# Two GpSimd copies moved behind a subtraction, and wider warm-up products on TensorE, in an attention and expert-layer kernel

## The chip, the cores and the metric

The kernel runs on one core of one Trainium2 chip. The metric is the time of one execution on the device in microseconds (us). The kernel before took 209.54 us, the median of three runs (209.17 to 210.24). One further execution was recorded by the hardware profiler: it took 208.29 us, of which 206.5 us lie between its first and its last instruction (the span). All places in time below are counted from the start of that span.

## The reference, cut to what matters

```python
B, H, S, Ns, D = 8, 8, 512, 32, 64
scores  = x @ state^T / 8                 # per batch and head: 512 x 32
a       = exp(scores - max) / sum         # over the 32 states
xread   = a @ state                       # 512 x 64
scores2 = state @ x^T / 8                 # 32 x 512
a2      = exp(scores2 - max) / sum        # over the 512 positions
sread   = a2 @ x                          # 32 x 64
h       = concat(xread, sread)            # 544 rows, heads side by side: 512 wide
out     = gelu(h @ w_in) @ w_out          # 512 -> 2048 -> 512
```

The result has 8 x 544 rows of 512 float32 values.

## The kernel before

The eight batches follow one another, and in each the work of the next one is prepared. TensorE (PE in the profile) is fed in program order. The kernel folds `state @ w_in` into a matrix P, so that `gelu` takes P times the transposed attention weights (`mm1`). The second product of each batch, gelu times `w_out`, is done by Strassen's scheme: seven half-size products, named "3", "4", "5", "1", "2", "7", "6" in the order in which they run, with sums and differences before (`g_sum`) and after them.

Three parts matter here. The first is the combination behind the products. [...]

```python
def c22(b):
    xs[b, "v"] = c_tile("v")
    o = xs[b, "o", 1]
    nc.gpsimd.tensor_tensor(out=xs[b, "v"], in0=xs[b, "q"], in1=o[:, :, :NH], op=ALU.subtract)  # L588
    nc.vector.tensor_tensor(out=o[:, :, NH:], in0=xs[b, 3], in1=xs[b, "v"], op=ALU.add)         # L591, reads bank 3
    x_out(b, 1)

def X(b, name):
    bank = {"3": 0, "4": 1, "5": 0, "2": 1, "1": 2, "6": 3, "7": 2}[name]
    ...                                     # sixteen products into the bank (L569)
    elif name == "5":
        nc.scalar.copy(out=o, in_=ps)                                                           # L615
        nc.gpsimd.tensor_tensor(out=xs[b, "u"], in0=xs[b, "s34"], in1=o, op=ALU.subtract)       # L618
    elif name == "2":
        nc.scalar.copy(out=xs[b, "o", 1][:, :, :NH], in_=ps)                                    # L620
        c22(b)
    elif name == "1":
        nc.vector.tensor_tensor(out=xs[b, "q"], in0=ps, in1=xs[b, "s34"], op=ALU.add)           # L624
    elif name == "7":
        nc.vector.tensor_tensor(out=xs[b, "o", 0][:, :, :NH], in0=ps, in1=xs[b, "u"], op=ALU.add)  # L626, reads bank 2
```

The second part is GpSimd's copies of x. Each batch needs x in two arrangements: `x4` (`rearr`, L219), whose transpose feeds the scores, and `xo` (`rearr_ones`, L229), x with columns of ones between, so that one product gives both the sum of `a2` and `a2 @ x` (`sread`). There are two `xo` tiles: batch b uses `xos[b % 2]`. `hold_for` is a copy of one column that only keeps a following load from being issued early.

```python
def rearr_ones(b):
    A = atts[b]
    eng = nc.vector if b < 2 else nc.gpsimd
    src = xbs[b].rearrange("p (t c) (j d) -> p t c j d", t=2, d=D)
    for t in range(2):
        eng.tensor_copy(out=A.xo[:, :, :, 2 + 64 * t:66 + 64 * t].rearrange("p j c d -> p c j d"),
                        in_=src[:, t])                                                          # L229
```

The loop over batches has eight steps p in each:

```python
for b in range(2, B):
    nb = b + 1
    for p in range(8):
        k = 16 * b + 2 * p
        ...
        if p == 7 and nb < B:
            srt(b)                          # a transpose on TensorE (L403), reads srm
        M(k, k + 1)                         # mm1 (L460), each followed by gelu on ScalarE (L467)
        if b == 2 and p in (0, 3):
            pmat(2, 2 + p // 3)             # P of batch 2: products L416
        if p < 5:
            ...
            X(b - 1, "45127"[p])            # the products of the batch before
            if p < 3:
                g_sum(b - 1, "127"[p])
        if p == 0 and b + 3 < B:
            hold_for(b, 0)
            load_x(4 if b == 2 else b + 3)
        if p == 2 and b == 2:
            rearr_ones(3)                   # the line that moves
        if p == 6 and b == 2:
            hold_for(b, 12)
            load_x(5)
        if p == 0 and nb + 1 < B:
            begin(nb + 1)
            rearr(nb + 1)
        ...
        if p == 5:
            g_sum(b, "6")
            sread(b)                        # (L379) reads xo of batch b
            p_run(nb, (0, 1), ((0, 1), (3, 2)))  # P of the next batch: L416 into banks 0, 1, then 3, 2; then four copies to SBUF (L427, L428)
            sread_out(b)                    # L392, L393: writes srm
            if nb + 1 < B:
                rearr_ones(nb + 1)
        if p == 6:
            X(b, "3")
        if p == 7:
            p_run(nb, (2, 3), ((1, 2), None))
            X(b, "6")
```

The third part is the warm-up. At seven places of the first 11 us TensorE multiplies a tile of zeros by itself, to stay busy while it has nothing to do; nobody reads the result. The calls ask for 31, 3, 2, 2, 2, 12 and 3 products.

```python
warm = persist.tile([128, 128], BF16, name="warm")
nc.vector.memset(warm, 0.0)                 # L92

def keep_warm(n):
    ps = otile([128, 512], "warm_ps")
    for _ in range(n):
        nc.tensor.matmul(ps[:, 0:128], lhsT=warm, rhs=warm, start=True, stop=True)   # L147
```

Of the kernel before, what the change touches and what calls it, by code (L numbers as in the profile page):

```python
# [10 lines left out]
BF16 = mybir.dt.bfloat16  # L11
# [6 lines left out]
def kernel(  # L18
# [8 lines left out]
    nc = tc.nc  # L27

    B, H, S, D = x.shape
    _, _, NS, _ = state.shape  # L30
# [8 lines left out]
    persist = ctx.enter_context(tc.tile_pool(name="persist", bufs=1))  # L39
# [15 lines left out]
    def otile(shape, name, at=None):  # L55
        if at is None:
            at = turn[0] % 4
            turn[0] += 1
        return ps_o.tile(shape, FP32, name=name, tag=f"o{at}")
# [17 lines left out]
    sb0 = persist.tile([128, 2, 2, 2, NS], BF16, name="sb0")  # L77
    gate = persist.tile([128, HC], FP32, name="gate")
    hold = persist.tile([128, 1], BF16, name="hold")
    warm = persist.tile([128, 128], BF16, name="warm")  # L80
    xos = [persist.tile([128, SJ, HC, 132], BF16, name=f"xo_{i}") for i in range(2)]
    x4s = [persist.tile([128, SJ, HC, 128], BF16, name=f"x4_{i}") for i in range(2)]

# [59 lines left out]

    def keep_warm(n):
        ps = otile([128, 512], "warm_ps")
        for _ in range(n):
            nc.tensor.matmul(ps[:, 0:128], lhsT=warm, rhs=warm, start=True, stop=True)  # L147


    def state_prep(b0, b1):  # L150
# [73 lines left out]
# [5 lines that stand above are left out]
            eng.tensor_copy(  # L229
                out=A.xo[:, :, :, 2 + 64 * t:66 + 64 * t].rearrange("p j c d -> p c j d"),  # L230
                in_=src[:, t],
            )
# [37 lines left out]
    def xtr_dma(b):  # L270
        A = atts[b]
        nc.sync.dma_start_transpose(
            out=A.xT.rearrange("p j c n -> p (j c) n"),
            in_=A.x4.rearrange("p j c n -> p (j c n)"),
        )
# [41 lines left out]
    def scores(b, half):  # L317
        A = atts[b]
        if half == 0:
            begin_e(b)  # L320
        pt = ps_f.tile([128, SJ, 2, 2, NS], FP32, name="pt", tag="f")
        for ci in range(2):
            c = 2 * half + ci
            for j in range(SJ):
                nc.tensor.matmul(  # L325
                    pt[:, j, :, ci, :],
                    lhsT=A.xT[:, j, c, :],
                    rhs=sbd[:, b, c, :],
                    start=True,
                    stop=True,  # L330
                )
        nc.scalar.activation(
            out=A.e[:, :, 64 * half:64 * half + 64],
            in_=pt.rearrange("p j t c n -> p (j t) (c n)"),
            func=AF.Exp,
            scale=scale,
        )

    def norm(b, half):
        A = atts[b]  # L340
        G = SJ * 2
        hs = slice(64 * half, 64 * half + 64)
        e4 = A.e[:, :, hs].rearrange("p g (c n) -> p g c n", n=NS)
        cs = att.tile([128, G, 2], FP32, name="cs", tag="cs")
        nc.vector.reduce_sum(out=cs, in_=e4, axis=AX.X)  # L345
        ics = att.tile([128, G, 2], FP32, name="ics", tag="ics")
        nc.vector.reciprocal(out=ics, in_=cs)  # L347
        nc.vector.tensor_tensor(  # L348
            out=A.a[:, :, hs].rearrange("p g (c n) -> p g c n", n=NS),
            in0=e4,  # L350
            in1=ics[:, :, :].to_broadcast((128, G, 2, NS)),
            op=ALU.mult,
        )
# [11 lines left out]
    def atr_dma(b):  # L365
        A = atts[b]
        A.AT = att.tile([128, SJ, 2, 128], BF16, name="AT", tag="AT")
        nc.sync.dma_start_transpose(
            out=A.AT.rearrange("p j t n -> p (j t) n"), in_=A.a
        )  # L370
# [29 lines left out]
    def srt(b):  # L400
        A = atts[b]
        ps = ps_f.tile([128, HC, NS], BF16, name="srT", tag="f")
        nc.tensor.transpose(  # L403
            ps.rearrange("p c n -> p (c n)"), A.srm.rearrange("q t d -> q (t d)"), ident
        )
        nc.vector.tensor_copy(out=XSR[:, :, :, b], in_=ps)  # L406
# [3 lines left out]
    def p_mm(b, f, tiles):  # L410
        if b not in Ps:
            Ps[b] = att.tile([128, 2, d_ff], BF16, name="P", tag="P")
        ps = [tiles([128, 512], "p_ps") for t in range(2)]
        for c in range(HC):
            for t in range(2):
                nc.tensor.matmul(  # L416
                    ps[t][32 * c:32 * c + 32, :],
                    lhsT=sbd[64 * t:64 * t + 64, b, c, 32 * t:32 * t + 32],
                    rhs=w_in_bf[64 * t:64 * t + 64, c, f * 512:(f + 1) * 512],
                    start=True,  # L420
                    stop=True,
                )
        return ps
# [6 lines left out]
    def pmat(b, f):  # L430
        p_copy(b, f, p_mm(b, f, ftile))
# [347 lines left out]
    def p_run(b, fs, banks, copy=None):  # L779
        done = []  # L780
        for f, at in zip(fs, banks):
            it = iter(at or ())
            tiles = (lambda shape, name: otile(shape, name, next(it))) if at else ftile
            done.append((b, f, p_mm(b, f, tiles)))
        for x in done:
            (copy or p_copy)(*x)
# [5 lines left out]
    def hold_for(b, m):  # L792
        nc.gpsimd.tensor_copy(out=hold, in_=gs[b][:, m, 0:1])


    def M(*ms):
        for m in ms:
            mm1(m // MC, m % MC)
# [5 lines left out]
    begin(0)  # L804
    begin_e(0)
    keep_warm(31)
    cast0(0)
    st0 = state0()
# [38 lines left out]
    for ms in ((0, 1), (2, 3)):  # L847
        for t in range(2):
            for m in ms:
                nc.tensor.matmul(  # L850
                    hps[m],
                    lhsT=Ps[0][:, t, m * 128:(m + 1) * 128],
                    rhs=atts[0].AT[:, :, t, :],
                    start=(t == 0),
                    stop=(t == 1),
# [81 lines left out]
# [4 lines that stand above are left out]
            if p == 1 and nb < B:  # L941
                scores(nb, 0)
                scores(nb, 1)
            if p in (2, 3) and nb < B:
                norm(nb, p - 2)
            if p == 3 and nb + 1 < B:
                xtr_dma(nb + 1)
            if p == 5 and nb < B:
                atr_dma(nb)
            if p == 7 and nb < B:  # L950
                srt(b)
                if nb == B - 1:
                    srt(nb)
            M(k, k + 1)
            if b == 2 and p in (0, 3):
                pmat(2, 2 + p // 3)
            if b == 2 and p == 1:
                w_sums(4)
            if p < 5:
                if p == 0:  # L960
                    g_sum(b - 1, "5")
                X(b - 1, "45127"[p])
                if p < 3:
                    g_sum(b - 1, "127"[p])
            if nb == B and p < 4:
                for m in range(4 * p, 4 * p + 4):
                    mm1_sr(m)
            if p == 0 and b + 3 < B:
                hold_for(b, 0)
                load_x(4 if b == 2 else b + 3)  # L970
            if p == 2 and b == 2:
                rearr_ones(3)
            if p == 6 and b == 2:
                hold_for(b, 12)
                load_x(5)
# [3 lines that stand above are left out]
            if nb == B:  # L979
                if p == 4:  # L980
                    r_homes()
                    r_sum("5")
                    r_sum("2")
                if p == 5:
                    g_sum(b, "6")
                    R("3")
                    r_sum("1")
                    R("4")
                    r_sum("6")
                    r_sum("7")  # L990
                if p == 6:
                    R("5")
                    X(b, "3")
                    R("2")
                    R("1")
                if p == 7:
                    R("6")
                    X(b, "6")
                continue
            if p == 5:  # L1000
                g_sum(b, "6")
                reads = (b, nb) if nb == B - 1 else (b,)
                for r in reads:
                    sread(r)
                p_run(nb, (0, 1), ((0, 1), (3, 2)))
                for r in reads:
                    sread_out(r)
                if nb + 1 < B:
                    rearr_ones(nb + 1)
            if p == 6:  # L1010
                X(b, "3")
            if p == 7:
                p_run(nb, (2, 3), ((1, 2), None))
                X(b, "6")
    b = B - 1
# [40 lines left out]
```

The softmax here doesn't subtract the row's maximum and nothing guards it: scores larger than these inputs give would overflow.

## Time and profile before

| | before |
|---|---|
| time, median of three runs | 209.54 us |
| span of the profiled execution | 206.5 us |
| mean granted TensorE clock | 0.998 |
| GpSimd copies L229 (to `xo`) | 12, 1279 ns mean, 15.0 us |
| GpSimd differences L618 (`u`), L588 (`v`) | 6 each, 1493 and 1402 ns mean |
| chain that ended last, share of PE | 82% |

A line of a timeline reads: start, duration, engine, line of the kernel, operation, tile written <- tiles read, shape, and xN where N equal instructions stand together; a bracket at the end gives the idle time of the engine before it and what ended it. A line of the waits reads: who waited, for whom, us in total, times, longest. Matmuls are pipelined: the duration of a group of them includes the last one's way through the array, so two groups can overlap, and the time that a group costs TensorE is read from its start to the start of the next group. DVE is VectorE, ACT is ScalarE, POOL is GpSimd, PEld is TensorE's weight load.

### The profile page before, as it was taken

How to read it: one execution, taken by the hardware profiler on the slowest of the kernel's cores; microseconds unless marked ns; L12 is line 12 of the kernel's file. 1: busy time of each engine (PE TensorE's matmuls, PEld its weight loads, DVE VectorE, ACT ScalarE, POOL GpSimd, SP SyncE). 2: the span in 40 equal slices, each digit the busy share in tenths (PEclk: the TensorE clock that was granted, in tenths of full speed). 3: DMA queues.
4: the chain of work that ended last, by engine and by line, in shares of the span. 5: the costliest groups of instructions: out<-in, count | busy, mean ns of one | idle time of the engine just before them, and what ended most of it. 6: DMA issues, size and time to landing. Idle time of an engine off the chain costs nothing.

```text
span 206.5 us, 4827 instructions
## 1 busy us (share of the span) xinstructions
PE 198.2 (96%) x2022; PEld 136.1 (66%) x2027; DVE 142.3 (69%) x227; ACT 134.2 (65%) x242; POOL 69.1 (33%) x74
## 2 busy tenths in 40 slices
PE   8699999999999899999999999999999999999992
PEld 7445444455667467766776677577765887878891
DVE  2954886997795868976797767765778533183971
ACT  3864877798885569666967596678758376744020
POOL 8964303724259605370627502520220020200000
PEclk9999999999999999999999999999999999999999
DMA  6999999697358687751783606340115000030134
GB/s 203 183 176 204 206 198 200 139 186 155 44 110 105 203 105 103 153 170 36 85 172 129 77 3 141 122 97 0 56 68 138 0 23 31 0 152 3 51 115 144
DMA packets 40535, 23.16 MB, mean 112 GB/s; under 512 B 21825, under 2 KB 39105, under 8 KB 40513
## 3 DMA queue, kind: packets, MB, share of 16 engines
q0 software_dynamic: 13952, 8.10, 28.7%
q1 hardware_dynamic: 25872, 14.36, 27.6%
q10 hardware_dynamic: 688, 0.39, 0.6%
q8 instruction: 16, 0.26, 0.5%
q14 instruction: 7, 0.05, 0.1%
HBM read 17.30 MB, written 8.91 MB: 127 GB/s over the span
## 4 chain that ended last, share of the span: by engine, by line
PE 82%; POOL 5%; DVE 5%; issue 3%; DMA 2%; ACT 1%; SPq 0%; POOLq 0%; DVEq 0%; ACTq 0%
PE xp L569 35%; PE hp L460 23%; PE p_ps L416 4%; PE hps L501 3%; PE op L514 3%; PE op L486 3%; PE rp L745 3%; DMA x0f<-in_x_dram 2%; PE xp L675 2%; PE pt L325 1%; POOL xo L229 1%; POOL x L219 1%; POOL u L618 1%; PE sr L379 1%; DVE P L428 1%
## 5 line engine op out<-in xcount | busy, mean ns | idle before, releaser
L467 ACT ACTIVATE g<-hp 128x512 bf16<-128x512 f32 x124 | 67.3, 604 | 28.4 <-PE hp L460 21.4
L460 PE MATMUL hp<-AT,P 128*128 128x512 bf16 x248 | 63.6, 379 | 0.0
L569 PEld LDWEIGHTS <-gsum 128*128 128x128 bf16 x528 | 51.2, 98 | 13.1 <-issue 2.1
L563 DVE TENSOR_TENSOR gsum<-g 128x2048 bf16<-128x2048 bf16 x35 | 45.5, 1317 | 0.1
L569 PE MATMUL xp<-ws,gsum 128*128 128x256 bf16 x304 | 36.3, 273 | 0.0
L460 PEld LDWEIGHTS <-P 128*128 128x128 bf16 x248 | 22.9, 98 | 19.9 <-issue 2.8
L569 PE MATMUL xp<-ws,g 128*128 128x256 bf16 x224 | 26.8, 273 | 0.0
L569 PE MATMUL xp<-w_out_bf,gsum 128*128 128x256 bf16 x224 | 26.6, 273 | 0.0
L428 DVE CAST P<-p_ps 128x512 bf16<-128x512 f32 x30 | 19.6, 684 | 8.7 <-PE p_ps L416 8.6
L569 PEld LDWEIGHTS <-g 128*128 128x128 bf16 x224 | 21.8, 98 | 5.1 <-issue 0.2
L618 POOL TENSOR_TENSOR u<-s,oh 128x512 f32<-128x512 f32 x6 | 9.0, 1493 | 41.1 <-ACT oh L615 41.1
L427 ACT CAST P<-p_ps 128x512 bf16<-128x512 f32 x30 | 16.9, 600 | 5.7 <-PE p_ps L416 5.4
L219 POOL COPY x<-xb 128x1024 bf16<-128x1024 bf16 x12 | 13.6, 1163 | 15.8 <-DMA xb<-in_x_dram 15.8
L229 POOL COPY xo<-xb 128x1024 bf16<-128x1024 bf16 x12 | 15.0, 1279 | 4.6 <-PE sr L379 4.6
L588 POOL TENSOR_TENSOR v<-q,oh 128x512 f32<-128x512 f32 x6 | 8.4, 1402 | 20.6 <-ACT oh L620 20.6
L416 PE MATMUL p_ps<-w_in_bf,sbd 64*32 64x512 bf16 x248 | 11.9, 384 | 0.8 <-DVE oh L591 0.4
L591 DVE TENSOR_TENSOR oh<-xp,v 128x512 f32<-128x512 f32 x6 | 4.2, 692 | 11.8 <-POOL v L588 11.8
L612 DVE TENSOR_TENSOR s<-xp,s 128x512 f32<-128x512 f32 x6 | 4.1, 691 | 11.3 <-PE xp L569 11.3
L348 DVE TENSOR_TENSOR a<-e,ics 128x512 bf16<-128x512 bf16 x14 | 10.4, 743 | 0.6 <-DVE ics L347 0.2
L624 DVE TENSOR_TENSOR q<-xp,s 128x512 f32<-128x512 f32 x6 | 4.1, 684 | 7.8 <-PE xp L569 7.8
L345 DVE TENSOR_REDUCE cs<-e 128x16 f32<-128x512 bf16 x14 | 9.5, 675 | 0.0
L406 DVE COPY XSR<-srT 128x128 bf16<-128x128 bf16 x8 | 5.7, 758 | 5.2 <-PE srT L403 5.2
(111 smaller groups left out, 225.3 us busy)
## 6 DMA issues: line engine op xcount, KB each, us to landing
out_dram<-oh SPq DMA_DIRECT2D x15, 256.0 KB, 2.4
xb<-in_x_dram POOLq DMA_DIRECT2D x7, 512.0 KB, 6.0
out_dram<-oh SPq DMA_DIRECT2D x6, 512.0 KB, 2.8
w_out_bf<-in_moe_w_out_dram POOLq DMA_DIRECT2D x4, 512.0 KB, 11.8
w_in_bf<-in_moe_w_in_dram POOLq DMA_DIRECT2D x6, 256.0 KB, 11.6
out_dram<-osb SPq DMA_DIRECT2D x5, 256.0 KB, 3.1
x0f<-in_x_dram SPq DMA_DIRECT2D x3, 256.0 KB, 3.9
w_in_bf<-in_moe_w_in_dram POOLq DMA_DIRECT2D x4, 128.0 KB, 4.0
```

The source lines that it names most:

```text
L219: nc.gpsimd.tensor_copy(out=A.x4[:, :, :, 64 * t:64 * t + 64].rearrange("p j c d -> p c j d"), in_=src[:, t],)
L229: eng.tensor_copy(out=A.xo[:, :, :, 2 + 64 * t:66 + 64 * t].rearrange("p j c d -> p c j d"), in_=src[:, t],)
L345: nc.vector.reduce_sum(out=cs, in_=e4, axis=AX.X)
L348: nc.vector.tensor_tensor(out=A.a[:, :, hs].rearrange("p g (c n) -> p g c n", n=NS), in0=e4, in1=ics[:, :, :].to_broadcast((128, G, 2, NS) ...
L416: nc.tensor.matmul(ps[t][32 * c:32 * c + 32, :], lhsT=sbd[64 * t:64 * t + 64, b, c, 32 * t:32 * t + 32], rhs=w_in_bf[64 * t:64 * t + 64, c ...
L427: nc.scalar.copy(out=dst[:, 0, :], in_=ps[0])
L428: nc.vector.tensor_copy(out=dst[:, 1, :], in_=ps[1])
L460: nc.tensor.matmul(hp, lhsT=Ps[b][:, t, m * 128:(m + 1) * 128], rhs=atts[b].AT[:, :, t, :], start=(t == 0), stop=(t == 1),)
L467: nc.scalar.activation(out=gs[b][:, m, :], in_=hp, func=AF.Gelu)
L563: nc.vector.tensor_tensor(out=t, in0=g_q(b, h0, k0), in1=g_q(b, h1, k1), op=op)
L569: nc.tensor.matmul(ps[:, j - js[0], :], lhsT=lhs[:, m, 128 * j:128 * j + 128], rhs=rhs[:, m, :], start=(first and j == js[0] and m == 0), ...
L618: nc.gpsimd.tensor_tensor(out=xs[b, "u"], in0=xs[b, "s34"], in1=o, op=ALU.subtract)
```

## The change

It has two independent parts. The first gives GpSimd's two `xo` copies of the second batch's stage (b = 2 in the loop) other places in its program. The copies for batch 3 stood between `u` and `v`; they now stand behind `v`, where those for batch 4 stood. Those for batch 4 go to the last step of the stage, behind the issue of the load of batch 5's x. In the stages from b = 3 on the order stays. The purpose is that GpSimd computes `v` as soon as its inputs are there. The second part makes the zero tile 512 wide and does four warm-up products of 128 columns as one of 512 columns (with 384 or 256 where fewer are left): 55 products become 16, each with its own weight load, at an unchanged number of columns.

```diff
-    warm = persist.tile([128, 128], BF16, name="warm")
+    warm = persist.tile([128, 512], BF16, name="warm")
...
     def keep_warm(n):
         ps = otile([128, 512], "warm_ps")
-        for _ in range(n):
-            nc.tensor.matmul(ps[:, 0:128], lhsT=warm, rhs=warm, start=True, stop=True)
+        while n > 0:
+            w = 128 * min(n, 4)
+            nc.tensor.matmul(
+                ps[:, 0:w], lhsT=warm[:, 0:128], rhs=warm[:, 0:w], start=True, stop=True
+            )
+            n -= 4
...
-            if p == 2 and b == 2:
-                rearr_ones(3)
...
                 for r in reads:
                     sread_out(r)
-                if nb + 1 < B:
+                if b == 2:
+                    rearr_ones(3)
+                elif nb + 1 < B:
                     rearr_ones(nb + 1)
             if p == 6:
                 X(b, "3")
             if p == 7:
+                if b == 2:
+                    rearr_ones(4)
                 p_run(nb, (2, 3), ((1, 2), None))
```

## The prediction

> **What bounds the kernel now.** I read the page's busy shares first, then the list of what TensorE itself waited for, then the timelines of the stage in which those waits lie.
>
> ```profile
> PE 198.2 (96%) x2022; PEld 136.1 (66%) x2027; DVE 142.3 (69%) x227; ACT 134.2 (65%) x242; POOL 69.1 (33%) x74
> ```
>
> TensorE is busy for 96% of the span. What can be won without taking work from it is its idle time. The list of waits with TensorE as the waiter has seven lines; these three lie behind the start-up:
>
> ```profile
> PE p_ps L416 <- DVE oh L591: 0.4, 1, 0.4
> ...
> PE p_ps L416 <- DVE oh L626: 0.2, 1, 0.2
> PE srT L403 <- DVE srm L393: 0.2, 1, 0.2
> ```
>
> All three happen once, so it is not a matter of every batch. L591 reads `v`, which GpSimd makes (L588). GpSimd's timeline in that stage (b = 2, from 51.46 us):
>
> ```profile
> 61.37 2.23 POOL L618 TENSOR_TENSOR u<-s,oh 128x512 f32<-128x512 f32 x1
> 63.56 2.47 POOL L229 COPY xo<-xb 128x1024 bf16<-128x1024 bf16 x2
> 65.99 1.27 POOL L588 TENSOR_TENSOR v<-q,oh 128x512 f32<-128x512 f32 x1
> 67.23 2.03 POOL L229 COPY xo<-xb 128x1024 bf16<-128x1024 bf16 x2
> ```
>
> There is no idle time ahead of `v`: it started at 65.99 because two copies stood before it, not because an input was missing. Its inputs came earlier: `q` at 61.10 (L624, 60.42 + 0.68), and the copy L620 at 64.04 in ScalarE's timeline:
>
> ```profile
> 63.46 0.58 ACT L620 COPY oh<-xp 128x512 f32<-128x512 f32 x1 [1.06 <-PE xp L569]
> ```
>
> What the late `v` costs is read on VectorE and TensorE. VectorE first:
>
> ```profile
> 67.30 0.69 DVE L591 TENSOR_TENSOR oh<-xp,v 128x512 f32<-128x512 f32 x1 [2.54 <-POOL v L588]
> ```
>
> VectorE stood still for 2.54 us, and everything behind L591 in its order came late. TensorE in the same stage:
>
> ```profile
> 67.19 0.41 PE L416 MATMUL p_ps<-w_in_bf,sbd 64*32 64x512 bf16 x8
> 68.04 0.37 PE L416 MATMUL p_ps<-w_in_bf,sbd 64*32 64x512 bf16 x1 [0.44 <-DVE oh L591]
> 68.64 0.41 PE L416 MATMUL p_ps<-w_in_bf,sbd 64*32 64x512 bf16 x7 [0.23 <-DVE oh L626]
> 68.98 1.04 PE L460 MATMUL hp<-AT,P 128*128 128x512 bf16 x4
> 69.85 1.91 PE L569 MATMUL xp<-ws,g 128*128 128x256 bf16 x16
> 71.98 0.23 PE L403 MATMUL srT<-ident,srm 128*128 128x128 bf16 x1 [0.23 <-DVE srm L393]
> 72.05 1.03 PE L460 MATMUL hp<-AT,P 128*128 128x512 bf16 x4
> ```
>
> The same steps one batch later (b = 3), where no copy stands before `v`:
>
> ```profile
> 90.15 0.63 PE L416 MATMUL p_ps<-w_in_bf,sbd 64*32 64x512 bf16 x16
> 90.71 1.04 PE L460 MATMUL hp<-AT,P 128*128 128x512 bf16 x4
> 91.59 1.91 PE L569 MATMUL xp<-ws,g 128*128 128x256 bf16 x16
> ...
> 93.39 1.03 PE L460 MATMUL hp<-AT,P 128*128 128x512 bf16 x4
> ```
>
> Here the sixteen L416 products run without a break. Behind 75 us no wait of TensorE appears in its list at all, so a gain in b = 2 should reach the end.
>
> [...]
>
> **Part one: the GpSimd copies.** No instruction is added or removed.
>
> Step 1: `v` starts when L620 has ended. In b = 3 it started 0.09 us after L620's end (86.47 + 0.58 = 87.05, `v` at 87.14), so here at 64.04 + 0.09 = 64.13. It takes 1.27 to 1.68 us (the spread over the batches) and ends at 65.4 to 65.8. L591 follows 0.04 us later and takes 0.69: done by 66.1 to 66.6.
>
> Step 2: L626 reads the bank of product "7", whose matmuls end at 64.13 + 1.91 = 66.04. It follows L591 and ends at about 66.8 to 67.2. TensorE wants bank 3 at 67.19 + 0.34 = 67.53 (eight L416 products take 0.34 us start to start in the same stage). Both banks are free by then, and both waits go.
>
> Step 3, the gain on TensorE: from the first L416 to the next L460 it is 68.98 - 67.19 = 1.79 us now, against 90.71 - 90.15 = 0.56 in b = 3. This gives **1.23 us**, nearly twice the 0.67 that the list of waits shows, because the list counts from the modelled end of a product and not from when the next could have started.
>
> Step 4, the transpose L403: from L569 to the L460 behind the transpose it is 72.05 - 69.85 = 2.20 us, against 93.39 - 91.59 = 1.80: **0.40 us** more. With the change TensorE would be there at 71.98 - 1.23 - 0.40 = 70.35. VectorE must have `srm` by then: sum L563 from 66.8 to 67.2 on, 1.22 us alone and 1.82 against a GpSimd copy (the one now at 68.50), two copies of P 1.2, reciprocal and `srm` 0.5. Its middle is 67.0 + 1.5 + 1.2 + 0.5 = 70.2. That is narrow; at the worst, 67.2 + 1.82 + 1.7 = 70.7, some 0.35 us of the 0.40 stays.
>
> Step 5: the copies in their new places. Those of batch 3 run from about 65.5 to 67.5, those of batch 4 behind the load of batch 5, which waits for a gelu that moves up with TensorE. That load was issued at 70.86, now at about 69.6, and takes 0.9 us to issue, so the copies run from 70.5 to 72.5. [...] Batch 3's `xo` is read at 89.80, batch 4's another 21 us on: nothing waits for them.
>
> Cross-check: the stage b = 2 takes 75.32 - 51.46 = 23.86 us, b = 3 takes 96.66 - 75.32 = 21.34. Of the 2.52 between, two `pmat` calls that only b = 2 has cost 0.44 each (from 51.46 to the L569 at 52.76 is 1.30, less 0.86 for four L460). The rest, 1.64, is the 1.23 + 0.40 above. Sum of part one: **-1.63 us**, chosen in full since steps 1 to 3 have 0.3 to 0.7 us to spare.
>
> **Part two: the warm-up.** The columns stay 55 x 128. VectorE clears the tile first:
>
> ```profile
> 0.82 0.11 DVE L92 MEMSET warm<- 128x64 uint32 x1 [0.82 <-PEq L1040]
> ```
>
> 64 words take 0.11 us; the memset L98 behind it takes 0.17 for 128, so 256 take an estimated 0.17 + 2 x 0.06 = 0.29: TensorE starts 0.18 us later. [...] The first real products (L174, now at 4.41) waited for ScalarE's `st_bf` until 4.27; the last zero product would clear the array at 4.28 + 0.18 = 4.46. So 0.05 to 0.15 us are lost there. What follows hides it: the second slice of x arrives at 5.12, and the chain then passes through GpSimd's product L310 at 9.37, ahead of which GpSimd issues loads without a gap from 3.00 on, while the reciprocal that L310 reads was ready at 8.54, 0.8 us early. [...] Sum of part two: **0.0 us**, between -0.1 and +0.15; I put +0.03.
>
> 209.54 - 1.63 + 0.03 = 207.94, which I round to 207.9.
>
> **The rivals.** (a) VectorE takes over as the bound of the same steps: `srm` still comes late, as step 4's narrow sum allows, or the moved copies slow the sum L563 in front of the P copies. For it: L563 took 1.82 us against a copy. Against it: b = 3 has a copy at 90.19 with `srm` done at 92.87, 0.46 before TensorE asks. It would make 208.3. (b) The copies of batch 4, now late, delay the load of batch 6 or batch 5's arrangement L219. For it: they stand in one queue. Against it: about 2.7 us lie between their end and the next hold at 76.82 - 1.6. It would give back 0.5 us at most: 208.4. [...] (d) The gap isn't there in ordinary runs, and nothing changes: 209.5. Against it: it comes from program order alone.
>
> **Range and chances.** The mechanism fixes about 1.6 us; (a) and (b) take 0.3 to 0.5 off; the runs of the kernel before are themselves 1.07 us apart. I choose 207.0 to 209.0. Two per cent is 4.2 us, under 205.35 or over 213.7: far more than any step here moves. Faster 0.02, same 0.97, slower 0.01.
>
> **What would show it.** In the profile after: `v` of b = 2 at about 64.1 directly behind L620, with both `xo` copies behind it; no wait of L416 for L591 or L626; 0.56 us from L416 to L460; the transpose without a wait; stage b = 2 at some 22.2 us, the later ones at 21.3; the start-up's first L514 still near 13.5. The prediction is wrong if the stage shrinks and the time doesn't, if a new wait appears in TensorE's list, or if the start-up moves by over 0.3 us.

## The result and the profile after

The changed kernel takes 206.89 us (median of four runs, 206.85 to 207.77) against 209.35 us before (four runs, 208.53 to 210.24). The ratio is 0.9892, with a 95% interval of 0.9843 to 0.994: faster by 0.6 to 1.6%, and so within 2%. The point predicted, 207.9, was 1.0 us too high, and the measured median lies 0.1 us below the range. The gain is about 2.3 to 2.5 us where 1.6 was worked out.

The waits of TensorE in the profile after (who waited for whom, us in total, times, longest):

```profile
PE warm_ps L148 <- DVE warm L92: 1.2, 1, 1.2
PE pt L329 <- DMA xT<-x: 0.9, 1, 0.9
PE aT_ps L366 <- POOL a L314: 0.5, 1, 0.5
PE op L490 <- DMA w_out_bf<-in_moe_w_out_dram: 0.3, 1, 0.3
```

The three waits of the stage b = 2 are gone. A new one has come: the scores of batch 2 (L329) wait 0.9 us for a transpose made by DMA. All lines of the kernel behind the warm-up have numbers larger by 4 or so than before. GpSimd's timeline in the stage b = 2, which starts at 52.61 here, 1.15 us later than in the profile before:

```profile
63.05 2.23 POOL L622 TENSOR_TENSOR u<-s,oh 128x512 f32<-128x512 f32 x1
65.28 1.67 POOL L592 TENSOR_TENSOR v<-q,oh 128x512 f32<-128x512 f32 x1
66.90 2.01 POOL L233 COPY xo<-xb 128x1024 bf16<-128x1024 bf16 x2
...
71.98 2.03 POOL L233 COPY xo<-xb 128x1024 bf16<-128x1024 bf16 x2
```

`v` follows `u` directly, and 0.08 us behind ScalarE's copy L624 (64.61 + 0.59 = 65.20). TensorE in the same stage:

```profile
68.33 0.62 PE L420 MATMUL p_ps<-w_in_bf,sbd 64*32 64x512 bf16 x16
68.89 1.04 PE L464 MATMUL hp<-AT,P 128*128 128x512 bf16 x4
69.76 1.91 PE L573 MATMUL xp<-ws,g 128*128 128x256 bf16 x16
71.65 0.23 PE L407 MATMUL srT<-ident,srm 128*128 128x128 bf16 x1
71.72 1.03 PE L464 MATMUL hp<-AT,P 128*128 128x512 bf16 x4
```

From the L420 products to the next L464 it is 0.56 us instead of 1.79. The stage takes 74.99 - 52.61 = 22.38 us instead of 23.86.

The two profiles, cut into stretches, show that this isn't all:

| stretch | before | after | difference |
|---|---|---|---|
| start to the first product with `w_out` | 13.45 us | 13.28 us | -0.17 |
| from there to stage b = 2 | 38.01 | 39.33 | +1.32 |
| stage b = 2 | 23.86 | 22.38 | -1.48 |
| from b = 3 to the end of the last VectorE sum | 127.50 | 127.50 | 0.00 |
| from there to the end of the span | 3.69 | 2.61 | -1.08 |

Of the 1.32 us lost ahead of the stage, 0.94 are the wait for the transpose and 0.3 a wait for `w_out`. The last line was not foreseen at all: after the last sum only output transfers are left, and no line of the change touches them. What differs there is in the DMA view. The last half microsecond of TensorE's work in the kernel before, 202.0 to 202.5 us (DMA queue, kind: packets, MB, share of 16 DMA engines):

```profile
q1 hardware_dynamic: 126, 0.14, 76.2%
q8 instruction: 1, 0.02, 11.6%
```

Beside the outputs on q1 lies one packet of instructions; 11.6% of 16 engines for 0.5 us is 0.93 us of one engine. The issue of the last three outputs on SyncE's queue, before:

```profile
201.09 2.68 SPq L634 DMA_DIRECT2D out_dram<-oh  x3
```

And after, where no packet of q8 comes behind 191 us:

```profile
200.75 1.83 SPq L638 DMA_DIRECT2D out_dram<-oh  x3
```

The outputs themselves land later, too: the first of these three, which had been issued in 0.38 us and 1.3 us ahead of the packet, and also the one that ScalarE issues (how many, KB each, us from issue to landing), before and after:

```profile
out_dram<-oh SPq DMA_DIRECT2D x1, 256.0 KB, 3.9
...
out_dram<-oh ACTq DMA_DIRECT2D x1, 64.0 KB, 2.5
```

```profile
out_dram<-oh SPq DMA_DIRECT2D x1, 256.0 KB, 2.3
...
out_dram<-oh ACTq DMA_DIRECT2D x1, 64.0 KB, 1.7
```

The profile counts the packets of q8, before and after:

```profile
q8 instruction: 16, 0.26, 0.5%
```

```profile
q8 instruction: 15, 0.25, 0.5%
```

They carry 16 KB each and move with TensorE's program: when the sixteenth comes, all 4049 instructions that the profile of before counts for TensorE have started, 253 to a packet on average. Such a packet is called a fetch from here on. 39 pairs fewer (a product and its weight load each) are 78 instructions of 4049, enough to do without the sixteenth fetch. The experiments ask whether a fetch costs time. Packets of instructions on another queue (q14, 8 KB) lie 2.3 to 2.5 us ahead of the end of the last VectorE sum before, after and in every experiment; they make no difference between the kernels.

### The profile page after: what moved, and what is told of

Read it like the earlier page. It is cut to its first block, busy times and chain, and to the rows that moved or that the text cites. A ratio compares the mean times of both kernels' runs of the same rounds, so it can differ in the third digit from the quotient of the medians.

```text
span 205.1 us, 4749 instructions
## 1 busy us (share of the span) xinstructions
PE 198.5 (97%) x1982; PEld 133.7 (65%) x1988; DVE 142.7 (70%) x227; ACT 134.3 (65%) x242; POOL 69.5 (34%) x74
## 4 chain that ended last, share of the span: by engine, by line
PE 79%; DMA 15%; POOL 5%; issue 0%; DVE 0%; POOLq 0%
PE xp L573 40%; PE hp L464 23%; DMA xb<-in_x_dram 11%; PE p_ps L420 4%; DMA xT<-x 4%; PE hps L505 3%; PE rp L749 3%; POOL w_in_bf L105 2%; PE xp L679 2%; PE pt L329 1%; PE sr L383 1%; POOL x L223 1%; PE op L490 1%; POOL sbd L95 1%; POOL w_out_bf L113 0%
## 5 line engine op out<-in xcount | busy, mean ns | idle before, releaser
L464 PE MATMUL hp<-AT,P 128*128 128x512 bf16 x248 | 63.4, 379 | 0.1
L464 PEld LDWEIGHTS <-P 128*128 128x128 bf16 x248 | 22.9, 98 | 19.7 <-issue 2.3
L592 POOL TENSOR_TENSOR v<-q,oh 128x512 f32<-128x512 f32 x6 | 9.0, 1494 | 20.4 <-ACT oh L624 17.2
L420 PE MATMUL p_ps<-w_in_bf,sbd 64*32 64x512 bf16 x248 | 11.4, 383 | 0.1
## 6 DMA issues: line engine op xcount, KB each, us to landing
w_in_bf<-in_moe_w_in_dram POOLq DMA_DIRECT2D x6, 256.0 KB, 11.6
```

The source lines that it names most:

```text
L420: nc.tensor.matmul(ps[t][32 * c:32 * c + 32, :], lhsT=sbd[64 * t:64 * t + 64, b, c, 32 * t:32 * t + 32], rhs=w_in_bf[64 * t:64 * t + 64, c ...
L464: nc.tensor.matmul(hp, lhsT=Ps[b][:, t, m * 128:(m + 1) * 128], rhs=atts[b].AT[:, :, t, :], start=(t == 0), stop=(t == 1),)
```

## The experiments

Three theories stood against each other. **A**: two gains, the stage b = 2 and an end without a fetch of instructions, where the place of the fetch is what matters. **B**: the copies bring everything and the shorter end is chance. **C**: fewer TensorE instructions are a gain as such. The first four kernels share 44 runs of the kernel before (median 209.27 us).

### The copies alone

```diff
 # the changed kernel, with the old warm-up
-    warm = persist.tile([128, 512], BF16, name="warm")
+    warm = persist.tile([128, 128], BF16, name="warm")
-        while n > 0:
-            w = 128 * min(n, 4)
-            nc.tensor.matmul(ps[:, 0:w], lhsT=warm[:, 0:128], rhs=warm[:, 0:w], start=True, stop=True)
-            n -= 4
+        for _ in range(n):
+            nc.tensor.matmul(ps[:, 0:128], lhsT=warm, rhs=warm, start=True, stop=True)
```

> Only the GpSimd copies move; the warm-up stays at 55 products of 128 columns, so TensorE's program is as long as before. Theory A (two separate gains: the stage b = 2 loses 1.5 us of waits, and the wide warm-up shortens the end of the span by 1.0 us because TensorE's sixteenth fetch of instructions no longer falls among the last output transfers): the stage is 22.2 to 22.4 us as with the whole change, a fetch of instructions still lies within the last 4 us, the span from the last VectorE sum to its end stays near 3.6 us, and the time is 1.3 to 1.7 us under the kernel before. Theory B (the copies bring everything, and the shorter end was chance): the time is 2.2 to 2.5 us under the kernel before, as with the whole change.

Measured: 207.45 us, ratio 0.990 (0.9868 to 0.9933), 1.8 us by the medians. The stage takes 22.23 us. The fetch is there, between 201.5 and 202 us, and the end takes 3.90 us. SyncE's last issues:

```profile
199.98 2.96 SPq L634 DMA_DIRECT2D out_dram<-oh  x3
```

They take 2.96 us as against 1.83 in the changed kernel: the shorter end doesn't come with the copies. The time fits A; the interval (1.4 to 2.8 us) doesn't exclude B by itself, the end of the span does.

### The wide warm-up alone

```diff
 # the kernel before, with the warm-up of the change; every rearr_ones stays where it was
-    warm = persist.tile([128, 128], BF16, name="warm")
+    warm = persist.tile([128, 512], BF16, name="warm")
-        for _ in range(n):
-            nc.tensor.matmul(ps[:, 0:128], lhsT=warm, rhs=warm, start=True, stop=True)
+        while n > 0:
+            w = 128 * min(n, 4)
+            nc.tensor.matmul(ps[:, 0:w], lhsT=warm[:, 0:128], rhs=warm[:, 0:w], start=True, stop=True)
+            n -= 4
```

> Only the warm-up is widened, the GpSimd copies stay where they were. Theory A: the stage b = 2 keeps its 23.9 us, no fetch of instructions lies in the last 4 us, the end from the last VectorE sum to the end of the span is 2.6 us instead of 3.6, and the time is 0.8 to 1.1 us under the kernel before. Theory B: within 0.2 us of the kernel before.

Measured: 208.79 us, ratio 0.998 (0.9964 to 0.9996), so 0.1 to 0.75 us of gain. The end takes 2.61 us without a fetch in it, as A says, 1.1 us less than before; yet the time gained is half of that. The wait for xT has about the size of the rest: this profile shows 1.0 us of it, and no profile of a kernel with the old warm-up shows any. In the changed kernel it reads so on TensorE:

```profile
40.98 0.64 PE L329 MATMUL pt<-sbd,xT 128*128 128x64 bf16 x16 [0.94 <-DMA xT<-x]
```

And its DMA view from 38.5 to 39.0 us:

```profile
q1 hardware_dynamic: 496, 0.12, 108.2%
q8 instruction: 1, 0.02, 12.1%
```

With fewer instructions ahead of it, the third fetch comes 5 us later than before (38.9 instead of 33.9 us) and begins as the last packets of the transpose move. The transpose took 7.3 us from its issue to its landing, as against 5.5 in the kernel before. The change took a fetch away from one place where something waits and put another into such a place.

### More instructions instead of fewer

```diff
 # the kernel before
-        for _ in range(n):
-            nc.tensor.matmul(ps[:, 0:128], lhsT=warm, rhs=warm, start=True, stop=True)
+        for _ in range(2 * n):
+            nc.tensor.matmul(ps[:, 0:64], lhsT=warm, rhs=warm[:, 0:64], start=True, stop=True)
```

> The kernel before with twice as many warm-up products of 64 columns: 55 pairs of TensorE instructions more than before, 110 rows, and the memset is as it was. Theory A (what counts is where the fetch falls, not how many instructions there are): the sixteenth fetch comes about 110 rows earlier, some 6 us at the 18 rows per us of the end, and so ahead of the last output transfers; the end is 2.6 us as with the whole change and the time 0.7 to 1.1 us under the kernel before although it issues more. Theory C (fewer instructions are the gain as such): 0.5 us or more over the kernel before. Theory B: as before.

Measured: 208.43 us, ratio 0.9953 (0.9929 to 0.9977): **faster with 110 instructions more**. The sixteenth fetch is at 196 us, the end takes 2.62 us, no wait for xT. This is A, and against B and C. The profile shows one thing more, on GpSimd and on TensorE:

```profile
60.16 2.48 POOL L219 COPY x<-xb 128x1024 bf16<-128x1024 bf16 x2 [5.33 <-DMA xb<-in_x_dram]
...
67.23 1.27 POOL L588 TENSOR_TENSOR v<-q,oh 128x512 f32<-128x512 f32 x1
```

```profile
69.28 0.37 PE L416 MATMUL p_ps<-w_in_bf,sbd 64*32 64x512 bf16 x1 [1.14 <-DVE oh L591]
```

The old order's wait is 1.14 us here and was 0.44 in the profile that the prediction used. GpSimd's chain to `v` begins when the load of batch 4's x lands, and that landing moves from run to run (GpSimd's L219 behind it starts 7.46 to 8.15 us into the stage in the five profiles of the old order).

### The larger memset alone

```diff
 # the kernel before
-    warm = persist.tile([128, 128], BF16, name="warm")
+    warm = persist.tile([128, 512], BF16, name="warm")
-            nc.tensor.matmul(ps[:, 0:128], lhsT=warm, rhs=warm, start=True, stop=True)
+            nc.tensor.matmul(ps[:, 0:128], lhsT=warm[:, 0:128], rhs=warm[:, 0:128], start=True, stop=True)
```

> The kernel before with the zero tile 512 wide and its products still 128 columns: the larger memset alone. All theories: TensorE begins 0.2 us later, the start-up hides it, and the time is within 0.3 us of the kernel before; a fetch still lies in the last 4 us. [...]

Measured: 209.28 us, ratio 0.999 (0.9969 to 1.0011). TensorE starts at 1.19 instead of 0.99 us, the first product with `w_out` comes at 13.28: the start-up hides it. The end takes 3.91 us with the fetch at 202.

The next four share twelve runs of the kernel before (median 209.20 us).

### The copies with the narrow warm-up

This is the changed kernel with the warm-up of the third experiment (and the small memset).

> The moved GpSimd copies with the narrow warm-up (110 products of 64 columns, the small memset): 94 pairs of TensorE instructions more than the changed kernel. Theory A (a fetch of 16 KB of TensorE's instructions costs about 1 us where it shares a DMA engine with a transfer that TensorE or the end waits for, and nothing elsewhere): the fetches fall at about 30, 41 and 196 us, clear of the transposes of batch 2's x (35 to 39 us) and of the last outputs; the end is 2.6 us, no wait of L325 for xT, and the time is 2.5 to 2.8 us under the kernel before, 0.2 to 0.6 under the changed kernel. Theory C (fewer instructions are the gain as such): 0.5 us or more over the changed kernel.

Measured: **205.92 us** (five runs, 205.89 to 206.19), ratio 0.9837 (0.9811 to 0.9863), the lowest median of all, with 188 TensorE instructions more than the changed kernel. The waits of TensorE:

```profile
PE warm_ps L147 <- DVE warm L92: 1.0, 1, 1.0
PE aT_ps L362 <- POOL a L310: 0.9, 1, 0.9
PE xT_ps L251 <- ACT x0b L237: 0.5, 1, 0.5
PE pc L286 <- DVE xT L255: 0.2, 1, 0.2
```

No wait is left behind the start-up. The fetches lie at 30, 43 and 193 us; the end takes 2.59 us:

```profile
199.97 1.83 SPq L634 DMA_DIRECT2D out_dram<-oh  x3
```

The gain is 3.3 us by the medians, more than the 2.8 expected at most.

### 21 pairs fewer

```diff
 # the changed kernel, but only the first group of warm-up products is widened
-            w = 128 * min(n, 4)
+            w = 512 if n >= 4 and asked == 31 else 128   # asked: the n of the call
-            n -= 4
+            n -= w // 128
```

> The moved copies, and only the first group of warm-up products widened, seven of 512 columns and three of 128: 21 pairs fewer than before, 18 more than the changed kernel. Theory A: the third fetch falls at about 36.5 us, among the transposes of batch 2's x, and the sixteenth still comes, some 2 us later than before (at about 203), among the last outputs: both are hit, the scores of batch 2 wait up to 1 us for xT, the end is 3.5 us or more, and the time is 0.5 to 1.2 us over the kernel with the copies alone although it issues fewer instructions. Theory C: between the kernel with the copies alone and the changed one.

Measured: 206.23 us (205.91 to 206.83), ratio 0.9848 (0.982 to 0.9876). The expectation failed: this kernel is faster than the copies alone, not slower. Its trace says why. With 4007 TensorE instructions the sixteenth fetch doesn't come at all (it does with 4049), so the end takes 2.62 us, and the fetch at 36.9 us costs the scores of batch 2 only 0.3 us. The rule of A for the end held, but the number of instructions at which the fetch comes had been misjudged; the rule for the transpose held with a smaller cost.

### 14 pairs more

```diff
 # the copies alone
-        for _ in range(n):
-            nc.tensor.matmul(ps[:, 0:128], lhsT=warm, rhs=warm, start=True, stop=True)
+        w = 64 if n in (2, 3, 12) else 128
+        if n == 12: n = 7                       # 14 halves instead of 12 products
+        for _ in range(n * 128 // w):
+            nc.tensor.matmul(ps[:, 0:w], lhsT=warm, rhs=warm[:, 0:w], start=True, stop=True)
```

> The moved copies, and the small groups of warm-up products cut into halves of 64 columns (the group of twelve shortened to fourteen halves): 14 pairs more than before, 28 rows. Theory A: the sixteenth fetch comes 1.5 us earlier than in the kernel with the copies alone, at about 200 us, ahead of the last three outputs; the third falls at about 33, ahead of the transposes; the end shrinks to 2.6 to 3.0 us and the time is 0.6 to 1.0 us under the kernel with the copies alone. Theory C: 0.1 us or more over it.

Measured: 207.85 us (205.99 to 208.48), ratio 0.9915 (0.9878 to 0.9953). The end is as expected: the fetch at 200.2 us, 3.4 us ahead of the end of the last sum, leaves an end of 2.67 us. The output issued 0.7 us ahead of it took 3.7 us to land as against 2.1 to 2.2 us in the thirteen other profiles, but nothing waits for that one. The 28 instructions more moved the fetch by 3 us against the last sum, not by the 1.5 expected. The time isn't as expected: one of the five runs took 205.99 us, the four others 207.72 to 208.48. The profiled execution, one of these four, lost 1.8 us elsewhere, in a wait for the load of the states, which took 8.6 us to land as against 5.4 to 7.4 in the other profiles. A fetch lies at 48.7 us, in the last 2.2 us of that load, as in no other profile; one profile can't say whether it was the cause.

### The changed kernel again, and four second profiles

> The changed kernel once more, beside the others of this call. Theory A: no fetch in the last 4 us, an end of 2.6 us, the third fetch at 38 to 40 us at the end of the transposes of batch 2's x, and a wait of the scores for xT of about 1 us, as in the first profile and as in the kernel with the wide warm-up alone; the time 2.0 to 2.5 us under the kernel before. If that wait was chance, it is gone here.

Measured: 206.60 us (205.90 to 207.89), ratio 0.9872 (0.9841 to 0.9903). The end takes 2.60 us. The expected wait for xT doesn't show, but it isn't disproved: the transpose took 5.9 us to land, at 40.30, beside a fetch at 39.7, while the start of this execution was 2.5 us late (first product with `w_out` at 15.76 us instead of 13.28), so that the scores came only at 41.92.

> A second profile of the wide warm-up alone. If the fetch of instructions decides: an end of 2.6 us without a fetch, a fetch at 38 to 40 us, and the scores of batch 2 waiting about 1 us for xT. If that wait was chance: none.

> A second profile of the copies alone. If the fetch decides: an end of 3.6 to 4.0 us with a fetch near 201, a fetch at about 34, and no wait for xT. If the longer end was chance: 2.6 to 3.0.

> A second profile of the copies with 21 pairs fewer. If the fetch decides: no sixteenth fetch, an end of 2.6 us, a fetch at about 36 us and a wait for xT of 0.3 us or more. If chance: anything between.

> A second profile of the copies with the narrow warm-up. If the fetch decides: an end of 2.6 us, fetches at about 30 and 42 us, no wait for xT, and some 206.0 us in all. If chance: a wait for xT or an end of 3.6 us may show.

Measured: the wide warm-up alone has an end of 2.61 us and a wait for xT of 0.5; the copies alone 3.71 us and none; 21 pairs fewer 2.62 us and 0.3; the copies with the narrow warm-up 2.62 us and none, 205.9 us in all.

### All fourteen profiles

| | last fetch | end of the span | fetch near 36 us | wait for xT |
|---|---|---|---|---|
| before | 202 us | 3.69 us | 33 us | none |
| larger memset | 202 | 3.91 | 33 | none |
| copies alone, twice | 201, 201 | 3.90, 3.71 | 34, 33 | none |
| 14 pairs more | 200 | 2.67 | 33 | none |
| narrow alone | 196 | 2.62 | 30 | none |
| copies and narrow, twice | 193, 193 | 2.59, 2.62 | 30, 30 | none |
| wide alone, twice | 193, 193 | 2.61, 2.61 | 39, 38 | 1.0, 0.5 us |
| changed kernel, twice | 190, 191 | 2.61, 2.60 | 38, 39 | 0.9, none |
| 21 pairs fewer, twice | 189, 188 | 2.62, 2.62 | 36, 36 | 0.3, 0.3 |

The end has two lengths and nothing between: 3.7 to 3.9 us with a fetch that begins within 0.2 us of the end of TensorE's work, 2.6 to 2.7 without. A wait for xT shows in five of the six profiles with a fetch between 36 and 40 us, and in none of the eight others. The landing of the transpose divides all fourteen: 4.8 to 5.5 us after its issue in these eight, 5.9 to 7.3 in the six.

The stage b = 2 sorts as cleanly. The middle column counts from the start of the stage to GpSimd's copy L219, which in the old order starts when the load of batch 4's x has landed (the trace names this load as the releaser in four of these five profiles, a VectorE sum in one):

| | stage start to L219 | stage b = 2 |
|---|---|---|
| old order: before | 7.46 us | 23.86 us |
| wide alone | 7.73 | 24.12 |
| larger memset | 7.75 | 24.14 |
| wide alone, second profile | 7.97 | 24.36 |
| narrow alone | 8.15 | 24.53 |
| new order, nine profiles | 7.76 to 7.99 | 22.23 to 22.38 |

In the old order the stage is the middle column plus 16.38 to 16.40 us, five times out of five: it hung on the landing of one load, microsecond for microsecond. In the new order it no longer does in six of the nine profiles: with a middle column of 7.76 to 7.83 us the stage takes 22.23 us. In the three with 7.93 to 7.99 it takes 22.34 to 22.38, about 14.4 us more than the middle column. The chain behind that load was shortened by 2.0 us; a late landing can still show.

## Why the prediction was right in part one and missed part two

- **Step 1** held: `v` started 0.08 us after the end of L624, the old L620, and took 1.67 us, the upper end of what was said.
- **Steps 2 and 3** held: both waits are gone and the L416 products need 0.56 us. Against the profile that was read this is the 1.23 us predicted.
- **Step 4** gave 0.24 of its 0.40 us in the first profile (2.20 to 1.96; `srm` was ready at 71.60, 0.1 us late), in most others all of it (stage 22.23). To that extent rival (a) came true, in the profile with the latest landing.
- **Step 5** held: nothing waits for the copies in their new places. **Rival (b)**, a load delayed by them, didn't show.
- **The term of part one was too small** for ordinary runs. The one profile had the earliest landing of all five with the old order. Their mean is 24.20 us, that of the nine with the new order 22.27: 1.9 us, not 1.63. With the landing of the profile that was read, the new order would by this table take its 22.23 us, and the gain would be 23.86 - 22.23 = 1.63, as worked out. The profiled execution was 1.25 us faster than the median (208.29 against 209.54), and the prediction did not ask which wait of the stage it had shortened. The cross-check could not see it either, as it used the same profile.
- **Part two failed**: no term of it stood for the instructions' way through the DMA. The -0.1 us at the lower end of its sum, put for the time that 39 fewer products save on TensorE, was the author's estimate; no run shows it. What the runs show of the 39 fewer is an effect on the fetches: 1.2 us gained at the end of the span (3.80 to 2.62, the means of four and ten profiles), and 0.3 to 1.0 us paid in the transposes in five of the six profiles with fewer instructions. A new wait in TensorE's list had been named as a sign that the prediction is wrong, and it came: this is where it is wrong. By itself, part two gained 0.4 us (0.1 to 0.75), where 0.0 had been put. What the prediction said of the memset (0.29 us estimated, 0.27 measured) and of its being hidden was right.
- **The sum**: 1.8 us for the copies alone and 0.5 for the wide warm-up alone, by medians, make 2.3 us, against 2.5 and 2.6 measured with both in the two series. That 207.9 was only 1.0 us off is in part luck: of the two effects that were missed, one gained 1.2 us and the other took up to 1.0 of it back.

## What to carry to other kernels

A wait that shows once, behind a chain that begins with a load, has the size of that load's luck in the one execution that was profiled (0.44 us in one profile of the old order here, 1.14 in another): look for what the chain hangs on, and take its spread, not its value. Where a program of thousands of TensorE instructions ends with small transfers, look in the DMA view for packets of instructions in the last microseconds; a few dozen instructions more or fewer ahead of them, here in the warm-up at the start, can move them (28 more moved the last one by 3 us here). Such a change can pay at one place and cost at another, so each place where a fetch now falls has to be looked at.

## What the runs showed of the hardware

- TensorE's instructions come in packets of 16 KB; the one at 202.4 us took some 0.93 us of one DMA engine. Where the sixteenth began within 0.2 us of the end of TensorE's work, the span was 1.2 us longer behind the last sum; where it began 3.4 us or more ahead of the end of that sum, or didn't come, it was not. Beside the fifteen others of the kernel before TensorE shows no wait; beside the one at the transpose in the changed kernel (38.9 us) it shows 0.9 us.
- In the four profiles with the long end the last outputs landed later: the one of 256 KB 3.9 to 4.2 us after its issue (2.3 to 2.9 in the ten others), the one that ScalarE issued 2.5 to 2.7 (1.6 to 1.7). SyncE also took longer over issuing the last three (2.68 to 2.96 us as against 1.82 to 1.85). The output of 256 KB had been issued in 0.38 us, 1.3 us or more ahead of the fetch, so the transfers were held up and not only an issue. By what way the fetch does this, these views don't tell; it stays open, as it wasn't tried apart from TensorE's program.
- TensorE gets faster during the start-up: in the profile of before one of the 31 first products starts every (3.49 - 0.314) / 30 = 0.106 us, one of the later 12 every (0.83 - 0.216) / 11 = 0.056 us (0.314 and 0.216 are the longest and the shortest duration of a single product in the view of the tile `warm`). Four transposes in a row at 4.7 to 5.1 us took 0.39 us before and with the larger memset, but 0.63 with the copies alone, whose warm-up is that of before: when TensorE gets faster differs between executions of the same warm-up. The granted clock at that place is 1.00 before and with the copies alone.
